# A windowed attention and a gated MLP on one core: GpSimd's loads put behind the last transposed x of a tile, key and query transposes a step later

## The chip, the core and the metric

The kernel runs on one core of a Trainium2 chip. The core has five engines with queues of their own: TensorE (PE, with its weight loads shown as PEld), VectorE (DVE), ScalarE (ACT), GpSimd (POOL) and SyncE (SP). Each executes its instructions in the order in which they were written; they meet through semaphores. GpSimd and SyncE also issue DMAs. The metric is the device time of one execution in microseconds. Before the change it is 281.39 us, the median of three runs between 280.98 and 281.63.

## What is computed

Windowed attention over 8 batches, 8 heads, 576 positions and 64 values a head, and then a two-layer MLP with the gate h * sigmoid(1.702 h) on its 4608 rows of 512:

```python
B, H, S, D = q.shape                      # 8, 8, 576, 64
scores = np.matmul(q, k.transpose(0, 1, 3, 2)) / np.sqrt(D)
mask = np.abs(pos[:, None] - pos[None, :]) <= 32
scores = np.where(mask, scores, -1e9)
attn = softmax(scores)
x = np.matmul(attn, v).transpose(0, 2, 1, 3).reshape(B * S, H * D)
h = x @ w_in                              # 512 -> 2048
out = (h * (1 / (1 + np.exp(-1.702 * h)))) @ w_out
```

Inputs and output are float32.

## The kernel before

The 4608 rows are cut into 36 units of 128 and 9 tiles of 512, so a tile is four units: tile t has units 4t to 4t+3. A unit's attention makes a row block x, and the MLP then works on a tile of x that is transposed (xT). Both MLP layers multiply 2x2 blocks with seven products in place of eight; `x_sums` makes the four sums of xT blocks that layer 1 needs, and `g_sums` those for layer 2. In `l1_group` product 1 reads a half of xT, and product 7, the next, reads the first sum that `x_sums` makes.

From tile 2 on the program is a loop over tiles, with `front(t)` and `back(t)` in turn; in both u = 4t + 4, the first unit of the tile behind.

- `front(t)` runs the scores of units u to u+3, the `x_sums` of tile t, and layer-2 work of the tile before.
- `back(t)` runs four groups (n = 0 to 3) of layer 1 of tile t, fills them with layer 2, and has the values of units u to u+3 in groups 1 and 3, with their division (`norm`) and their transposition into xT[t+1] (`x_T`, a DMA transpose that SyncE issues).

Everything that attention needs is loaded in `back` too, some units ahead, on two other queues:

- `fetch(u)` (GpSimd) issues the loads of q(u), k(u+1) and, from u = 18 on, v(u-1). The staging buffers of q and k are five deep, those of v nine. A load that crosses the end of a batch is issued in two pieces.
- `turn(u)` (SyncE) issues the DMA transposes of q(u) and k(u+1), which wait for those loads. The scores of unit u need q(u), k(u) and k(u+1) transposed.
- `spread(u)` (GpSimd) calls `odd_v(u)`, two copies that make a version of v shifted by 64 rows: the first takes the second half of v(u), the second the first half of v(u+1). The buffer `vo` that they write is one of three from unit 16 on, so the first copy waits for the values of unit u-3. The values of unit u need v(u) and this copy.

In each group the order of GpSimd's queue and of SyncE's is the order of these calls in `back`. For tile t > 3 it is, with one line a group:

```text
n=0: turn(u+4)  fetch(u+5)                          spread(u+2)
n=1: turn(u+5)  fetch(u+6)  x_T(u) x_T(u+1)         spread(u+3)
n=2: turn(u+6)  fetch(u+7)                          spread(u+4)
n=3: turn(u+7)  fetch(u+8)  x_T(u+2) x_T(u+3)       spread(u+5)
```

SyncE also issues the output stores, which come out of layer 2.

Of the kernel before, what the change touches and what calls it, by code (L numbers as in the profile page):

```python
# [17 lines left out]
F16 = mybir.dt.float16  # L18
# [5 lines left out]
TILE = 512  # L24


class _Kernel:
# [55 lines left out]
    def setup(self):  # L83
        nc, cst = self.nc, self.cst
        self.ident = cst.tile([128, 128], BF16, name="ident")
        self.identh = cst.tile([128, 128], F16, name="identh")
        self.mask = cst.tile([128, 4, SQ], BF16, name="mask")
        self.bias = cst.tile([128, 512], BF16, name="bias")
        self.w1 = cst.tile([128, 4, self.DFF], F16, name="w1")
        self.w2 = cst.tile([128, 16, self.DM], F16, name="w2")  # L90
        self.a = {i: cst.tile([128, 2, 1024], F16, name=f"a{i}") for i in (1, 2, 3, 4)}
        self.b = {i: cst.tile([128, 8, 256], F16, name=f"b{i}") for i in (1, 2, 3, 4)}
        self.k_first = cst.tile([128, 4, 64], BF16, name="k_first")
        self.v_first = cst.tile([64, self.H, 66], BF16, name="v_first")
        self.ve = [cst.tile([128, self.H, 66], BF16, name=f"ve{i}") for i in range(9)]
        self.vo = [cst.tile([128, self.H, 66], BF16, name=f"vo{i}") for i in range(5)]
        self.spark = cst.tile([128, 1], F32, name="spark")

    def setup_mask(self):

        D = self.work.tile([128, 128], F32, name="gap", tag="s7", bufs=2)
        self.nc.gpsimd.iota(D, pattern=[[-1, 128]], base=0, channel_multiplier=1,
                            allow_small_or_imprecise_dtypes=True)
        dve = self.nc.vector
        dve.tensor_single_scalar(self.ident, D, 0.0, op=ALU.is_equal)
        dve.tensor_copy(self.identh, self.ident)
        for r in (slice(0, 64), slice(64, 128)):
            d = D[r, r].rearrange("p (b s) -> p b s", b=1).to_broadcast([64, 2, SQ])
            up = int(r.start > 0)
            for blk, op in ((2 * up, ALU.is_ge), (2 - 2 * up, ALU.is_le)):  # L110
                dve.tensor_single_scalar(self.mask[r, blk:blk + 2, :], d, 0.0, op=op)
# [94 lines left out]
    def load_v(self, u, which=slice(None)):  # L206
# [3 lines left out]
        for off, b, s, n in list(self.pieces(128 * u, 128))[which]:  # L210
            self.nc.gpsimd.dma_start(t[off:off + n, :, :self.D], self.v[b, :, s:s + n, :].rearrange("h s d -> s h d"))  # L211

    def odd_v(self, u, eng, parts=(0, 1)):

        vo = self.vo[u % (3 if u > 15 else 5)]
        nxt = self.v_first if u == self.NU - 1 else self.ve[(u + 1) % 9][0:64]

        def words(ap):
            return ap.rearrange("p h d -> p (h d)").bitcast(I32)

        for i in parts:
            eng.tensor_copy(*((words(vo[64:128]), words(self.ve[u % 9][64:128])), (words(vo[0:64]), words(nxt)))[i])  # L222
# [88 lines left out]
    def values(self, u, tag):  # L311

        D = self.D
        p = self.p.pop(u)
        if tag == "t":
            acc = self.bank(tag, name="pv")
            self.acc[u] = [acc]
            acc = [acc[:, 0], acc[:, 1]]
        else:
            acc = [self.bank(x, name="pv") for x in tag]  # L320
            self.acc[u] = [x.rearrange("p (b n) -> p b n", b=1) for x in acc]
        for h in range(self.H):
            o = slice((h % 4) * (D + 1), (h % 4 + 1) * (D + 1))
            for blk in range(2):
                vt = (self.ve[u % 9], self.vo[u % (3 if u > 15 else 5)])[blk]
                w = p[:, h % 2, h // 2 * 2 + blk, :] if len(p.shape) == 4 else p[:, h % 2, h // 4, h // 2 % 2, blk, :]
                self.mm(acc[h // 4][64 * blk:64 * blk + 64, o], w, vt[:, h, :D + 1],
                        start=(h % 4 == 0))
# [423 lines left out]
    @staticmethod  # L752
    def do(fs, n=99):
        for _ in range(min(n, len(fs))):
            fs.pop(0)()
# [29 lines left out]
    def back(self, t):  # L785

        more = t + 1 < self.NT
        do, l2 = self.do, self.l2
        u = 4 * t + 4
        bands = [lambda i=i: self.band(u + i) for i in range(4)] if more else []  # L790
        dv = bands[0:2]
        for n in range(4):
            if (t, n) == (3, 1):
                self.turn(20)
            if (t, n) != (3, 0):
                self.turn(u + n + 4)
            if (t, n) not in ((2, 3), (3, 0), (3, 3)):
                self.fetch(u + n + 5)
            if t == 2 and n in (1, 3):
                self.values(u + n - 1, "t")  # L800
                self.norm(u + n - 1)
                self.x_T(u + n - 1)
            elif more and n in (1, 3):
                do(l2, self.AHEAD[n][0])
                self.values(u + n - 1, "AC")
                self.norm(u + n - 1)
                if u + n < self.NU - 1:
                    self.x_T(u + n - 1)
                self.values(u + n, "t")
                self.norm(u + n)  # L810
                self.x_T(u + n)
                do(l2, self.AHEAD[n][1])
            if (t, n) == (3, 0):
                self.fetch(20)
            self.spread(u + n + 2)
            if (t, n) == (3, 0):
                self.fetch(21)
            if (t, n) == (3, 3):
                self.fetch(24)

            key = ("first", n) if t == 2 else ("last", n) if not more else n
            share = dict(zip((1, 7, 2, 4), self.SHARES.get(key, (3, 3, 5, 5))))

            def fill(i):
                do(l2, share[i])
                self.l2eng = self.nc.scalar
                if t == 2 and n in (1, 3) and i == 7:
                    self.values(u + n, "t")
                    if n == 3:
                        self.norm(u + n)  # L830
                        self.x_T(u + n)
                if i == 4:
                    do(dv, 2 if (t, n) == (2, 2) else 99)

            def side(i):
                if (t, n, i) == (2, 1, 0):
                    self.norm(u + n)
                    self.x_T(u + n)
                else:
                    do(dv, 1)  # L840

            self.l1_group(t, n, fill, side)
            dv += bands[2:4] if n == int(t == 2) else []
            dv += self.g_sums(t, 2 * n, 2)
        return dv
# [132 lines left out]
```

## Time and profile before

| | |
|---|---|
| median of three runs | 281.39 us |
| the profiled execution | 281.27 us, of which the span from first to last instruction is 279.5 us |
| TensorE busy | 268.2 us (96% of the span) |
| VectorE, ScalarE busy | 210.9 us (75%), 195.4 us (70%) |
| GpSimd busy | 133.0 us (48%) |
| the chain that ended last | TensorE 90%, DMA 4%, GpSimd 3% |

The profile is one execution of the program, recorded by the hardware. Times are counted from the span's start. Views that group instructions show an engine, a line of the code, an operation and the tiles written and read (`vo<-ve`). A line can be that of a helper: every matmul has line 70. "Waits" lists how long an engine stood idle ahead of an instruction and what ended it. A DMA has a time of issue, which its queue spends, and a time "to landing", from its issue to its completion. TensorE's matmuls are pipelined, so that it counts as busy without gaps.

### The profile page before, as it was taken

The page shows a single profiled execution, that of the slowest core. Times are in us where ns is not written, and L with a number is a line of the kernel's source. Part 1 is how long each engine was busy: PE and PEld are TensorE (multiplying, and loading weights), DVE is VectorE, ACT ScalarE, POOL GpSimd, SP SyncE. Part 2 cuts the span into 40 slices and gives each one's busy share as a digit, 9 for nine tenths or more (in the row PEclk, how much of TensorE's full clock was granted, in tenths as well). Part 3 has the DMA queues.
Part 4 walks back from the last instruction along what each step waited for, and adds up shares of the span by engine and source line. Part 5 has one row for each costly group of instructions (what it writes and reads, how often), then busy time and mean ns, then how long its engine had stood idle before and what let it go on. Part 6 is the DMA issues. An engine that isn't in the chain of part 4 may idle for free.

```text
span 279.5 us, 8854 instructions
## 1 busy us (share of the span) xinstructions
PE 268.2 (96%) x3632; PEld 222.6 (80%) x3632; DVE 210.9 (75%) x491; ACT 195.4 (70%) x343; POOL 133.0 (48%) x199
## 2 busy tenths in 40 slices
PE   1989999999999999999999999999999999999995
PEld 1568656776888888888888888888888888888884
DVE  3454598897997798788888887888778887945731
ACT  2586893989897588758875877687759775568411
POOL 8894695999593554635684519442520100000000
PEclk9999999999999999999999999999999999999999
DMA  8999999999999999999999999999972050202023
GB/s 88 166 204 199 178 207 165 185 136 159 131 167 140 203 120 140 172 189 115 182 194 178 126 163 159 134 183 132 168 91 85 2 115 19 77 2 75 2 104 124
DMA packets 150265, 37.61 MB, mean 135 GB/s; under 512 B 138064, under 2 KB 145872, under 8 KB 150224
## 3 DMA queue, kind: packets, MB, share of 16 engines
q0 software_dynamic: 106656, 18.42, 95.5%
q1 hardware_dynamic: 43120, 18.10, 37.9%
q8 instruction: 28, 0.46, 0.7%
q10 hardware_dynamic: 448, 0.52, 0.6%
q14 instruction: 13, 0.11, 0.1%
HBM read 36.83 MB, written 9.44 MB: 166 GB/s over the span
## 4 chain that ended last, share of the span: by engine, by line
PE 90%; DMA 4%; POOL 3%; ACT 1%; issue 1%; POOLq 0%
PE o L70 41%; PE h L70 39%; PE pv L70 4%; DMA w<-in_moe_w_in_dram 4%; PE sc L70 3%; POOL ve L211 1%; POOL kq L152 1%; PE tp L201 1%; PE tp L244 1%; ACT p L279 1%; POOL w L125 1%; PE tp L368 0%; ACT kq L67 0%; PE tp L356 0%; ACT L692 0%
## 5 line engine op out<-in xcount | busy, mean ns | idle before, releaser
L471 ACT ACTIVATE g<-h 128x512 f16<-128x512 f32 x128 | 72.2, 598 | 35.0 <-PE h L70 34.8
L222 POOL COPY vo<-ve 64x264 int32<-64x264 int32 x71 | 32.7, 461 | 79.3 <-PE pv L70 52.0
L70 PEld LDWEIGHTS <-g 128*128 128x128 f16 x576 | 54.5, 98 | 10.1
L70 PE MATMUL h<-xs,a 128*128 128x256 f16 x384 | 57.6, 272 | 0.0
L70 PEld LDWEIGHTS <-a 128*128 128x128 f16 x512 | 49.5, 98 | 9.1
L70 PE MATMUL o<-w,g 128*128 128x256 f16 (+1 forms) x320 | 55.0, 294 | 0.0
L70 PEld LDWEIGHTS <-w 128*128 128x128 f16 x496 | 47.7, 98 | 7.6 <-DMA w<-in_moe_w_in_dram 0.2
L70 PE MATMUL h<-xT,w 128*128 128x256 f16 (+1 forms) x368 | 53.5, 277 | 0.1
L70 PEld LDWEIGHTS <-gs 128*128 128x128 f16 x384 | 36.7, 98 | 4.7
L70 PE MATMUL o<-b,g 128*128 128x256 f16 x256 | 38.3, 273 | 0.0
L70 PE MATMUL o<-b,gs 128*128 128x256 f16 x256 | 37.7, 273 | 0.0
L484 DVE TENSOR_TENSOR h<-h,s 128x512 f32<-128x512 f32 x32 | 22.4, 699 | 19.8 <-PE h L70 19.1
L211 POOL DMA_DIRECT2D ve<-in_v_dram x40 | 34.3, 864 | 5.6 <-DMA w<-in_moe_w_out_dram 2.1
L279 ACT ACTIVATE p<-sc 128x512 bf16<-128x512 f32 x64 | 32.8, 618 | 1.2 <-PE sc L70 1.0
L67 ACT COPY h<-h 128x512 f32<-128x512 f32 x32 | 18.8, 588 | 16.7 <-PE h L70 16.3
L340 DVE TENSOR_TENSOR x<-pv,rec 128x256 f16<-128x256 f32 (+1 forms) x52 | 27.4, 527 | 1.8
L141 POOL DMA_DIRECT2D qst<-in_q_dram x35 | 28.2, 809 | 0.3
L490 DVE TENSOR_TENSOR h<-h,s 128x512 f32<-128x512 f32 x32 | 22.4, 699 | 6.4 <-PE h L70 6.1
L141 POOL DMA_DIRECT2D kst<-in_k_dram x31 | 26.5, 855 | 0.8 <-DMA w<-in_moe_w_out_dram 0.8
L309 DVE TENSOR_TENSOR p<-p,mask 128x1024 bf16<-128x1024 bf16 x32 | 22.3, 696 | 0.2
L67 ACT COPY s<-h 128x512 f32<-128x512 f32 x32 | 19.2, 600 | 1.2
L70 PE MATMUL h<-xs,w 128*128 128x256 f16 x128 | 19.2, 273 | 0.0
(88 smaller groups left out, 343.2 us busy)
## 6 DMA issues: line engine op xcount, KB each, us to landing
out_dram<-o_sb SPq DMA_DIRECT2D x33, 256.0 KB, 4.6
ve<-in_v_dram POOLq DMA_DIRECT2D x32, 128.0 KB, 6.9
kst<-in_k_dram POOLq DMA_DIRECT2D x25, 128.0 KB, 6.5
qst<-in_q_dram POOLq DMA_DIRECT2D x21, 128.0 KB, 5.6
w<-in_moe_w_out_dram POOLq DMA_DIRECT2D x4, 512.0 KB, 11.0
w<-in_moe_w_in_dram POOLq DMA_DIRECT2D x3, 512.0 KB, 9.9
qst<-in_q_dram POOLq DMA_DIRECT2D x7, 96.0 KB, 5.7
kq<-in_q_dram POOLq DMA_DIRECT2D x2, 256.0 KB, 5.9
```

Of the source, the lines that this page charges most:

```text
L67: (eng.copy if eng is self.nc.scalar else eng.tensor_copy)(out, in_)
L70: self.nc.tensor.matmul(out, lhsT, rhs, start=start, stop=stop, skip_group_check=True)
L125: self.nc.gpsimd.dma_start(self.w1[:, :, lo:lo + n], self.w_in[:, lo:lo + n].rearrange("(k p) f -> p k f", p=128))
L141: self.nc.gpsimd.dma_start(t[off:off + n], src[b, :, s:s + n, :].rearrange("h s d -> s h d"))
L211: self.nc.gpsimd.dma_start(t[off:off + n, :, :self.D], self.v[b, :, s:s + n, :].rearrange("h s d -> s h d"))
L222: eng.tensor_copy(*((words(vo[64:128]), words(self.ve[u % 9][64:128])), (words(vo[0:64]), words(nxt)))[i])
L279: self.nc.scalar.activation(p[:, eo].rearrange("k h s -> k (h s)"), sc[eo], AF.Exp, scale=self.scale)
L309: (eng or self.nc.vector).tensor_mul(pv, pv, msk.to_broadcast([128, 8, 2, SQ]))
L340: dve.tensor_mul(x[:, 4 * at:4 * (at + n), :].rearrange("p (b h) d -> p b h d", b=n), acc[:, :, :, :D], r.to_broadcast([128, n, 4, D]))
L471: act.activation(g[:, f, 256 * half:256 * half + 256], bank.rearrange("p (i n) -> p i n", i=2), AF.Gelu_apprx_sigmoid)
L484: dve.tensor_add(e, b, s7)
L490: dve.tensor_add(c, b, s7)
```

## The change

A new one-element tile, `seen`, is written by GpSimd from the last column of xT[t], at the start of group 0 in `back(t)` for t > 2 as long as there are units to load. The copy waits for the last `x_T` of that tile, and everything behind it on GpSimd's queue follows it. Then come `fetch(u+4)` and `fetch(u+5)` together, and the other two fetches stand behind the `spread` of their group. On SyncE the transposes for unit u+4 move from group 0 to group 1, and those for u+5 stand behind x_T(u) and x_T(u+1). In tile 2 `fetch(19)` moves behind `spread(16)`. The special cases of tile 3 go. The odd buffers of units from 16 on are numbers 3, 4 and 0 in turn, where they were 0, 1 and 2. In the notation from above, for tile t > 2:

```text
n=0:            seen <- xT[t]  fetch(u+4) fetch(u+5)             spread(u+2)
n=1: turn(u+4)  x_T(u) x_T(u+1)  turn(u+5)                       spread(u+3)  fetch(u+6)
n=2: turn(u+6)                                                   spread(u+4)  fetch(u+7)
n=3: turn(u+7)  x_T(u+2) x_T(u+3)                                spread(u+5)
```

The orders of instructions on TensorE, VectorE and ScalarE stay as they were.

```diff
--- before.py
+++ after.py
@@ -95,6 +95,7 @@
         self.ve = [cst.tile([128, self.H, 66], BF16, name=f"ve{i}") for i in range(9)]
         self.vo = [cst.tile([128, self.H, 66], BF16, name=f"vo{i}") for i in range(5)]
         self.spark = cst.tile([128, 1], F32, name="spark")
+        self.seen = cst.tile([1, 1], F16, name="seen")
 
     def setup_mask(self):
 
@@ -210,9 +211,12 @@
         for off, b, s, n in list(self.pieces(128 * u, 128))[which]:
             self.nc.gpsimd.dma_start(t[off:off + n, :, :self.D], self.v[b, :, s:s + n, :].rearrange("h s d -> s h d"))
 
+    def odd(self, u):
+        return u % 5 if u < 16 else (3, 4, 0)[(u - 16) % 3]
+
     def odd_v(self, u, eng, parts=(0, 1)):
 
-        vo = self.vo[u % (3 if u > 15 else 5)]
+        vo = self.vo[self.odd(u)]
         nxt = self.v_first if u == self.NU - 1 else self.ve[(u + 1) % 9][0:64]
 
         def words(ap):
@@ -322,7 +326,7 @@
         for h in range(self.H):
             o = slice((h % 4) * (D + 1), (h % 4 + 1) * (D + 1))
             for blk in range(2):
-                vt = (self.ve[u % 9], self.vo[u % (3 if u > 15 else 5)])[blk]
+                vt = (self.ve[u % 9], self.vo[self.odd(u)])[blk]
                 w = p[:, h % 2, h // 2 * 2 + blk, :] if len(p.shape) == 4 else p[:, h % 2, h // 4, h // 2 % 2, blk, :]
                 self.mm(acc[h // 4][64 * blk:64 * blk + 64, o], w, vt[:, h, :D + 1],
                         start=(h % 4 == 0))
@@ -790,11 +794,9 @@
         bands = [lambda i=i: self.band(u + i) for i in range(4)] if more else []
         dv = bands[0:2]
         for n in range(4):
-            if (t, n) == (3, 1):
-                self.turn(20)
-            if (t, n) != (3, 0):
-                self.turn(u + n + 4)
-            if (t, n) not in ((2, 3), (3, 0), (3, 3)):
+            if t == 2 or n > 0:
+                self.turn(u + ((4, 5, 6, 7) if t == 2 else (0, 4, 6, 7))[n])
+            if t == 2 and n < 2:
                 self.fetch(u + n + 5)
             if t == 2 and n in (1, 3):
                 self.values(u + n - 1, "t")
@@ -810,13 +812,15 @@
                 self.norm(u + n)
                 self.x_T(u + n)
                 do(l2, self.AHEAD[n][1])
-            if (t, n) == (3, 0):
-                self.fetch(20)
+            if t > 2 and n == 0 and u + 4 <= self.NU:
+                self.nc.gpsimd.tensor_copy(self.seen, self.xT[t][0:1, 0, TILE - 1:TILE])
+                self.fetch(u + 4)
+                self.fetch(u + 5)
+            if t > 2 and n == 1:
+                self.turn(u + 5)
             self.spread(u + n + 2)
-            if (t, n) == (3, 0):
-                self.fetch(21)
-            if (t, n) == (3, 3):
-                self.fetch(24)
+            if n == 2 or t > 2 and n == 1:
+                self.fetch(u + n + 5)
 
             key = ("first", n) if t == 2 else ("last", n) if not more else n
             share = dict(zip((1, 7, 2, 4), self.SHARES.get(key, (3, 3, 5, 5))))
```

## The prediction

> **What bounds the kernel now.** I read the waits of TensorE first, then the busy time by tile, then the queues of GpSimd and SyncE around one tile, and last the landing times of single transfers. These are all of TensorE's waits in the whole run:
>
> ```profile
> PE tp L177 <- DVE ve L623: 6.3, 1, 6.3
> PE tp L356 <- ACT p L300: 0.8, 1, 0.8
> PE tp L356 <- DVE x L340: 0.4, 2, 0.3
> PE sc L70 <- DVE kq L67: 0.2, 1, 0.2
> ```
>
> All four name lines of the opening. In the tiles where the change stands, TensorE waits for nothing. The busy times by tile, cut from one tile's first score matmul to the next tile's (columns: stretch, its length, then busy time and count for each engine, granted clock, DMA share, GB/s), say the same:
>
> ```profile
> core 0: us, PE busy (x) PEld busy (x) DVE busy (x) ACT busy (x) POOL busy (x), PEclk, DMA share, GB/s
> ...
> 128.02:155.66 27.64, 27.64 (x385) 23.90 (x384) 23.31 (x56) 20.69 (x37) 16.88 (x26) 1.00 2.28 168
> ...
> 210.94:238.58 27.64, 27.64 (x386) 24.16 (x386) 22.98 (x56) 20.69 (x37) 0.81 (x2) 1.00 0.23 54
> ```
>
> A tile takes 27.64 us with the DMA rings crowded (2.28) and with them nearly empty (0.23). So what the change might relieve, loads and transposed x on the same rings, costs TensorE nothing today. The change can only lose, by letting something arrive after TensorE wants it. What it wants in the front of a tile (t = 5; columns: start, length, engine, line, operation):
>
> ```profile
> 155.66 0.70 PE L70 MATMUL sc<-qT,kT 64*64 64x64 bf16 x48
> ...
> 158.58 0.70 PE L70 MATMUL sc<-qT,kT 64*64 64x64 bf16 x48
> ...
> 161.41 0.60 PE L70 MATMUL h<-xs,a 128*128 128x256 f16 x4
> ```
>
> ```profile
> 160.16 0.42 DVE L400 TENSOR_TENSOR xs<-xT 128x512 f16<-128x512 f16 x1
> ```
>
> Call 155.66 the tile's zero. The last two units' scores start at +2.9. Product 7 reads the first x_sum at +5.75. That sum takes 0.42 and needs all of xT, so the last transposed x has to land by about +5.2 (0.1 for the hand-over).
>
> **The change part by part.** Units 20 to 23 are tile 4's back, u = 20. Before, GpSimd runs ahead of the tiles: `fetch(25)` to `fetch(28)` alternate with `spread(22)` to `spread(25)`, and each `spread` needs a v that was issued one `fetch` earlier. After, for t > 2, GpSimd's queue reads: `seen` (waits for the last transposed x of xT[t]), `fetch(u+4)`, `fetch(u+5)`, `spread(u+2)`, `spread(u+3)`, `fetch(u+6)`, `spread(u+4)`, `fetch(u+7)`, `spread(u+5)`, next `seen`. The second copy of `spread(u+3)` reads v(u+4), which is the very last load issued in front of it; that of `spread(u+4)` reads v(u+5), issued just before; and so on. So `fetch(u+6)` can't start before v(u+4) has landed, nor `fetch(u+7)` before v(u+5). On SyncE `turn(u+7)` still stands ahead of the transposes of x(u+2) and x(u+3), and its second DMA waits for k(u+8) out of `fetch(u+7)`. The last x then releases the next `seen`. Behind `seen` stand all later loads and odd copies, for which SyncE's transposes and TensorE's values wait; behind a late x_sum stand VectorE's copies of layer 2, which TensorE wants in the same front. That is a closed loop from tile to tile: last x, two loads, v lands, loads, v lands, loads, k lands, transposes, last x. Its length L, beside 27.64 us, decides.
>
> Queue costs today. GpSimd:
>
> ```profile
> 143.03 0.51 POOL L222 COPY vo<-ve 64x264 int32<-64x264 int32 x1 [0.29 <-DMA ve<-in_v_dram]
> 143.49 0.89 POOL L141 DMA_DIRECT2D qst<-in_q_dram  x1
> 144.37 0.88 POOL L141 DMA_DIRECT2D kst<-in_k_dram  x1
> 145.23 0.90 POOL L211 DMA_DIRECT2D ve<-in_v_dram  x1
> ...
> 167.29 1.35 POOL L141 DMA_DIRECT2D qst<-in_q_dram  x2
> ```
>
> SyncE:
>
> ```profile
> 147.54 1.26 SPq L235 DMA_TRANSPOSE qT<-qst  x1
> 148.90 1.21 SPq L235 DMA_TRANSPOSE kT<-kst  x1
> 151.42 2.54 SPq L352 DMA_TRANSPOSE xT<-x  x2
> ```
>
> A load costs GpSimd 0.87 (143.49 to 144.37), a q or k that crosses a batch 1.35; the copy that follows a landing holds the queue 0.46 (143.03 to 143.49), with 0.12 for the wake-up 0.58. SyncE spends 1.3 on a transpose.
>
> Landing times, each from a view of one tile cut to a few us: v in the opening's burst of loads; v with little else in flight; then one v issued at 125.5 among transposes; and one k issued at 140.5.
>
> ```profile
> L211 POOL DMA_DIRECT2D ve<-in_v_dram x5: 730/896/911, 5.2 to 8.6; - x5
> ...
> DMA to landing us min/median/max: 6.2/6.5/6.7
> ```
>
> ```profile
> L211 POOL DMA_DIRECT2D ve<-in_v_dram x2: 876/890/903, 45.8 to 48.4; - x2
> ...
> DMA to landing us min/median/max: 5.2/5.4/5.6
> ```
>
> ```profile
> DMA to landing us min/median/max: 7.5/7.5/7.5
> ```
>
> ```profile
> DMA to landing us min/median/max: 5.2/5.2/5.2
> ```
>
> Transposed x with no load in flight, and with loads:
>
> ```profile
> L352 SPq DMA_TRANSPOSE xT<-x x2: 1192/1204/1217, 206.7 to 208.0; - x2
> ...
> DMA to landing us min/median/max: 2.4/2.4/2.4
> ```
>
> ```profile
> L352 SPq DMA_TRANSPOSE xT<-x x2: 1192/1222/1251, 151.4 to 152.7; - x2
> ...
> DMA to landing us min/median/max: 4.6/5.9/7.1
> ```
>
> The loop of tile 4, from the landing of x(19). `seen` is a copy of one element; no row has it, it lies between nothing and the 0.46 of a copy, I take 0.25 with its wake-up. Five issues at 0.87 follow: v24 is issued at 4.6. It lands 6.0 later (between 5.2 and 7.5; it is the sixth of a burst, so nearer to 6.5 than to 5.2, with fewer loads in front than the opening had): 10.6. Copy, 11.2. q26 and k27, 12.9: v25 is issued and lands 5.5 later, a burst of three: 18.4. Copy, 19.0. q27, then k28 is issued at 19.9 and lands 5.2 later: 25.1. SyncE issues kT28 at 25.2, x(22) at 26.5, x(23) at 27.8. It lands 3.2 later (2.4 with clear rings; v26 is still in flight, against 7.1 with many loads): **L = 31.0**, 3.4 over the tile.
>
> Loads that cross a batch lengthen the other loops by 0.5 each before the loop's next step: k22 and q22 in tile 3, k31 and q31 in tile 5. In tile 3 the two output stores go out just ahead of the first loads, which I put at another 0.5. Tile 6 has one such v, but no k36; its last q has two pieces: 31.0 again. Tiles 3 to 6: 32.5 + 31.0 + 32.0 + 31.0 = 126.5, against 4 x 27.64 = 110.6. **15.9 over.** From tile 7 on only one v is left to load and nothing waits.
>
> The start has room. Before, x(15) lands here:
>
> ```profile
> 100.39 0.70 PE L70 MATMUL sc<-qT,kT 64*64 64x64 bf16 x48
> ```
>
> ```profile
> L352 SPq DMA_TRANSPOSE xT<-x x2: 1217/1241/1265, 96.4 to 97.7; - x2
> ...
> DMA to landing us min/median/max: 5.3/5.6/6.0
> ```
>
> That is 97.7 + 6.0 = 103.7, 3.3 after tile 3's zero of 100.39. After, the next loads, which today start while x(15) is in flight, come only behind it; I take 102.5, +2.1. It may land at +5.2, so 3.1 of the excess is free (1.9 if it lands as today). Loss: 15.9 - 3.1 = **12.8 us**. The profiled execution took 281.27 us (span 279.5), 0.12 under the median of 281.39: 281.27 + 12.8 = 294.1, forecast **294.0**. With the quickest landings shown (5.2, 5.2, 5.2, 2.4) L is 29.1 and the loss 118.9 - 110.6 - 3.1 = 5.2: 286.5. With the medians of today's whole run for all:
>
> ```profile
> ve<-in_v_dram POOLq DMA_DIRECT2D x32, 128.0 KB, 6.9
> kst<-in_k_dram POOLq DMA_DIRECT2D x25, 128.0 KB, 6.5
> ```
>
> and 5.9 for x, L is 37.3, 151.7 in all, and the loss 151.7 - 110.6 - 1.9 = 39: 320.
>
> The other edits cost nothing: the odd buffers rotate over three as before, and a copy into one waits for the values of three units earlier, which in tile 4 (20 and 21) run at 138.3, before the v that the copy needs lands. `fetch(19)` moves behind `spread(16)`, whose second copy waits for v17 until 88.2 (the chain of waits, then the queues of GpSimd and SyncE):
>
> ```profile
> 138.30 0.66 PE pv L70 x32
> ```
>
> ```profile
> 88.23 1.11 POOL L222 COPY vo<-ve 64x264 int32<-64x264 int32 x2 [2.84 <-DMA ve<-in_v_dram]
> ```
>
> ```profile
> 95.05 1.21 SPq L235 DMA_TRANSPOSE kT<-kst  x1
> ```
>
> k20 is then issued at 89.6 and lands at 95 (5.2) to 96, when SyncE wants it today: 0 to 1 us on x(15), which is part of the choice of 102.5. `turn(u+5)` behind x(u+1) is wanted only in the next tile.
>
> The Trainium skill ("DMA: Bandwidth & Descriptors", Anatomy of one DMA) gives a GpSimd load as 2.0 us plus its bytes at 436 GB/s: an estimate of 2.6 us for the 256 KB read here. By that L would be some 21 us and nothing would be lost; the whole-unit rows, 5.2 and up, disagree.
>
> **The rivals.**
> - *Loads land early enough* (not slower). L under 28.4 loses less than the 3.1 free: 281.3, no change. It needs three landings of 5.0 at most, x in 2.4 and no crossing cost. For it: landings today are stretched by transposes that will now stand apart. Against it: 5.2 with little else in flight.
> - *A gain.* x lands some 3 us sooner and VectorE no longer waits. An x_sum has waited for xT once in the run:
>
> ```profile
> DVE xs L400 <- DMA xT<-x: 0.4, 1, 0.4
> ```
>
> Even if all of that reached TensorE, which has no such wait, it would be 280.9.
> - *Crowded landings stay.* The loads of a tile are squeezed into less of it, two bursts meet the stores; nearer to the medians, L of 34 to 37: 305 to 320.
> - *The clock falls in the new gaps.* After the last matmul the rows show this:
>
> ```profile
> 276.20:278.60 2.40, 0.00 (x0) 0.00 (x0) 0.00 (x0) 0.33 (x1) 0.00 (x0) 1.00 0.54 177
> 278.70:279.40 0.70, 0.00 (x0) 0.00 (x0) 0.00 (x0) 0.00 (x0) 0.00 (x0) 0.50 0.04 12
> ```
>
> 2.6 us idle, then half clock. A stall of 3.4 us could do the same. If the slow time lasts as long as the stall, TensorE loses 1.7 us a tile; but the tile then takes 29.3, still under L, so the next stall shrinks by as much, and only the last one adds: 295.7. The Trainium skill ("TensorE: Matmul & The Clock Gate", What's actually happening) has half rate after an idle window of about 3.4 us, so by that rule gaps of this size are at the edge.
>
> **How the numbers follow.** Forecast with L of 29 to 34 (286 to 305): 0.66. Clock as well: 0.08. Crowded: 0.14. Loads early enough: 0.08. A gain: 0.04. About 0.2% is what a measurement of this kernel can tell from no change. So slower 0.88, same 0.08, faster 0.04. The range of 285 to 310 leaves out the last two cases and half of the crowded one.
>
> **What would show it.** Right: TensorE waits once a tile in the fronts of tiles 4 to 7, at product 7 or the last scores, some 2 to 5 us each, for VectorE's x_sum or a DMA; GpSimd waits for v two or three times a tile; tiles 3 to 6 take 30 to 33 us, tiles 7 and 8 as before. The forecast is wrong if the fronts show no wait, if v lands 4 us after issue, or if the last x goes out before k(u+8) has landed.

## The result, and the profile after

| | before | after |
|---|---|---|
| median (lowest to highest) of six runs | 281.23 us (280.98 to 281.63) | 297.15 us (296.46 to 301.14) |
| the profiled execution, its span | 281.27 us, 279.5 us | 296.56 us, 294.8 us |

The changed kernel takes 1.0563 of the time before, with a 95% interval of 1.0538 to 1.0588. Some executions take some per cent longer than the quickest of the same kernel; ratios leave them out, here and below, and where too few others are left, there is no ratio, and the median and range of all runs are given. The two profiled executions differ by 15.3 us in their spans, and this is the difference that the rest explains. From the page of the kernel after come TensorE's busy time and the chain that ended last, by engine:

```profile
PE 272.4 (92%) x3632; PEld 223.6 (76%) x3632; DVE 211.1 (72%) x491; ACT 196.4 (67%) x343; POOL 134.0 (45%) x204
...
PE 84%; DVE 6%; DMA 5%; ACT 2%; issue 2%; POOL 1%; SPq 0%; POOLq 0%; DVEq 0%
```

TensorE fell from 96% to 92% of the span, and the chain goes through other engines for 16% of it. The waits of TensorE between 100 and 262 us, where the kernel before had none, and GpSimd's of the whole run (us in total, times, the longest):

```profile
PE h L70 <- DVE xs L404: 5.7, 4, 1.9
PE sc L70 <- DMA qT<-qst: 2.3, 3, 1.0
PE sc L70 <- DMA kT<-kst: 2.3, 3, 1.0
PE sc L70 <- ACT p L283: 0.2, 1, 0.2
```

```profile
POOL vo L226 <- DMA ve<-in_v_dram: 52.6, 19, 5.1
POOL seen L816 <- DMA xT<-x: 26.5, 5, 5.6
POOL vo L226 <- PE pv L70: 8.8, 5, 3.3
```

TensorE waits for the first x_sum four times and for a transposed q or k three times each. GpSimd waits 52.6 us for values in flight and 26.5 at the new gate. Cut at each tile's first score matmul, tiles 3 to 6 read (stretch, length, busy time and count of PE, PEld, DVE, ACT and POOL, granted clock, DMA share, GB/s):

```profile
100.03:127.67 27.64, 27.64 (x385) 23.94 (x384) 23.46 (x57) 20.58 (x36) 14.79 (x22) 1.00 1.40 134
127.67:159.32 31.65, 28.42 (x385) 24.05 (x384) 23.13 (x56) 20.96 (x37) 15.03 (x24) 1.00 1.33 135
159.32:190.63 31.31, 28.42 (x385) 24.06 (x385) 23.07 (x56) 20.95 (x37) 13.98 (x22) 1.00 1.25 133
190.63:222.75 32.12, 30.09 (x386) 24.85 (x385) 23.47 (x56) 20.95 (x37) 15.15 (x24) 0.95 1.34 135
```

Tile 3 is as before. Tiles 4, 5 and 6 lose 4.0, 3.7 and 4.5 us against 27.64, together 12.2. Tile 3 starts 0.4 earlier than before (100.03, not 100.39), and the remaining 3.5 of the 15.3 fall behind 222.75, most of them in tile 7's front. The waits add up to only 10.5 us. Much of the rest stands as busy time: with the same number of matmuls a tile is busy for 28.42 where it was 27.64. No matmul is recorded longer for that (the mean of a 64x64 score matmul is 194 ns in both kernels' tile 4), but the records of neighbours overlap, and at a wait that overlap is missing: the 48 score matmuls that took 0.70 us in one go (158.58 before) take 0.45, 0.24 and 0.44 in three pieces below. In tile 6 the clock fell for a while as well (below). So a list of waits understates a stall. What a stall looks like, in tile 5's front (PE, then DVE; start, length, operation, and in brackets the idle time before it with what ended it):

```profile
162.24 0.45 PE L70 MATMUL sc<-qT,kT 64*64 64x64 bf16 x24
163.10 0.24 PE L70 MATMUL sc<-qT,kT 64*64 64x64 bf16 x2 [0.42 <-DMA qT<-qst]
163.98 0.44 PE L70 MATMUL sc<-qT,kT 64*64 64x64 bf16 x22 [0.63 <-DMA kT<-kst]
...
168.47 0.61 PE L70 MATMUL h<-xs,a 128*128 128x256 f16 x4 [1.76 <-DVE xs L404]
```

```profile
167.99 0.42 DVE L404 TENSOR_TENSOR xs<-xT 128x512 f16<-128x512 f16 x1 [4.10 <-DMA xT<-x]
```

Product 7 waits 1.76 us for a sum that VectorE starts at 167.99, as soon as the last transposed x is there. Before, that sum started 4.5 us behind its tile's zero; now it is 8.7 (167.99 less 159.32). Why x is late stands on GpSimd's queue (tile 4, then the gate of tile 5) and on SyncE's:

```profile
136.63 0.18 POOL L816 COPY seen<-xT 1x1 f16<-1x1 f16 x1 [5.63 <-DMA xT<-x]
137.12 0.89 POOL L142 DMA_DIRECT2D qst<-in_q_dram  x1 [0.31 <-issue]
...
141.46 0.93 POOL L212 DMA_DIRECT2D ve<-in_v_dram  x1
...
146.72 0.40 POOL L226 COPY vo<-ve 64x264 int32<-64x264 int32 x1 [2.43 <-DMA ve<-in_v_dram]
147.22 1.36 POOL L142 DMA_DIRECT2D qst<-in_q_dram  x2
...
149.43 0.91 POOL L212 DMA_DIRECT2D ve<-in_v_dram  x1
...
155.78 0.40 POOL L226 COPY vo<-ve 64x264 int32<-64x264 int32 x1 [4.99 <-DMA ve<-in_v_dram]
156.23 0.88 POOL L142 DMA_DIRECT2D qst<-in_q_dram  x1
157.10 0.89 POOL L142 DMA_DIRECT2D kst<-in_k_dram  x1
```

```profile
167.95 0.18 POOL L816 COPY seen<-xT 1x1 f16<-1x1 f16 x1 [4.96 <-DMA xT<-x]
```

```profile
161.65 1.19 SPq L239 DMA_TRANSPOSE kT<-kst  x1
162.93 2.53 SPq L356 DMA_TRANSPOSE xT<-x  x2
```

From one gate to the next it is 31.32 us (167.95 less 136.63), and each step starts where the one before it ends: gate, v issued at 141.46, its copy at 146.72, the next loads behind that copy, v issued at 149.43, its copy at 155.78, k issued at 157.10, its transpose at 161.65, the two x, gate. The gates stand at 103.40, 136.63, 167.95, 200.06 and 230.94, so 33.2, 31.3, 32.1 and 30.9 apart. TensorE needs 27.64 for a tile and follows.

### The profile page after: what moved, and what is told of

Its sections match the earlier page's. It is cut to its first block, busy times and chain, and to the rows that moved or that the text cites. A ratio compares the mean times of both kernels' runs of the same rounds, so it can differ in the third digit from the quotient of the medians.

```text
span 294.8 us, 8859 instructions
## 1 busy us (share of the span) xinstructions
PE 272.4 (92%) x3632; PEld 223.6 (76%) x3632; DVE 211.1 (72%) x491; ACT 196.4 (67%) x343; POOL 134.0 (45%) x204
## 4 chain that ended last, share of the span: by engine, by line
PE 84%; DVE 6%; DMA 5%; ACT 2%; issue 2%; POOL 1%; SPq 0%; POOLq 0%; DVEq 0%
PE h L70 37%; PE o L70 36%; DMA xT<-x 5%; PE pv L70 4%; PE sc L70 4%; DVE xs L404 1%; PE tp L178 1%; PE tp L202 1%; PE tp L248 1%; POOL kq L153 1%; DVE o L67 1%; ACT p L283 1%; DVE gs L419 1%; DVE o L568 1%; ACT p L304 1%
## 5 line engine op out<-in xcount | busy, mean ns | idle before, releaser
L70 PEld LDWEIGHTS <-g 128*128 128x128 f16 x576 | 54.8, 98 | 10.5
L70 PEld LDWEIGHTS <-a 128*128 128x128 f16 x512 | 48.9, 98 | 17.1 <-DVE xs L404 8.2
L226 POOL COPY vo<-ve 64x264 int32<-64x264 int32 x71 | 32.1, 453 | 64.0 <-DMA ve<-in_v_dram 52.6
L70 PE MATMUL o<-b,gs 128*128 128x256 f16 x256 | 38.5, 277 | 0.0
```

What stands on the lines that cost most here:

```text
L70: self.nc.tensor.matmul(out, lhsT, rhs, start=start, stop=stop, skip_group_check=True)
```

## The experiments

"Loss" below is the median less that of the kernel before in the same comparison.

**1. The changed kernel without its gate.**

```diff
-                self.nc.gpsimd.tensor_copy(self.seen, self.xT[t][0:1, 0, TILE - 1:TILE])
                 self.fetch(u + 4)
```

> The change without the copy that waits for the last x; GpSimd's loads follow one another as the change orders them. Closed loop: the link from x back to the loads is cut. GpSimd's own chain from one tile's first load to the next one's took 25.9 to 27.1 us in the changed kernel's trace, under the 27.64 of a tile, so nothing is lost: 281 to 283 us; if loads land later again because x flies among them, three landings of 7 us make that chain some 30 us and cost up to 8: at most 290. Rival, the parts add up (gate, order of loads, order on SyncE each with a share of the 15.9 us): about 292.

It took 299.7 us (294.03 to 303.24; before 281.98). The runs lie far apart, but the quickest of them is still 13 us above the quickest of the kernel before (281.07), and 2.4 below the quickest of the kernel after. So the gate isn't what most of the time hangs on. GpSimd's queue in tile 4:

```profile
134.29 0.92 POOL L212 DMA_DIRECT2D ve<-in_v_dram  x1
...
145.50 0.87 POOL L226 COPY vo<-ve 64x264 int32<-64x264 int32 x2 [7.03 <-PE pv L70]
146.32 1.36 POOL L142 DMA_DIRECT2D qst<-in_q_dram  x2
...
148.54 0.90 POOL L212 DMA_DIRECT2D ve<-in_v_dram  x1
...
155.49 0.67 POOL L226 COPY vo<-ve 64x264 int32<-64x264 int32 x1 [5.47 <-DMA ve<-in_v_dram]
156.11 0.88 POOL L142 DMA_DIRECT2D qst<-in_q_dram  x1
```

v(24) is issued 7 us earlier than in the kernel after (134.29, not 141.46), but the fetch at 146.32 starts hardly sooner (147.22 there): it stands behind copies that wait for an odd buffer, which TensorE's values free, and for v(24), issued at 134.29, which lands 10.1 us later by its record, at 144.4. The two waits end about a us apart, and which of them would hold it alone wasn't tried. So the loop closes another way: product 7, values, copy, loads, v lands, loads, k lands, x, product 7. Values in flight during a tile's work (104 to 200 us) show the price of the missing gate:

```profile
L212 POOL DMA_DIRECT2D ve<-in_v_dram x14: 707/901/935, 104.1 to 199.4; - x14
...
DMA to landing us min/median/max: 3.7/6.8/10.4
```

The same view of the kernel after:

```profile
L212 POOL DMA_DIRECT2D ve<-in_v_dram x13: 715/908/945, 105.6 to 190.2; - x13
...
DMA to landing us min/median/max: 3.7/4.5/6.4
```

With the gate loads and transposed x are apart and the median of a landing is 2.3 us lower, but GpSimd spends about 5 us idle at each gate. With or without it the tile is too short.

**2. Each fetch of groups 1 and 2 ahead of its spread,** the gate kept.

```diff
-            self.spread(u + n + 2)
             if n == 2 or t > 2 and n == 1:
                 self.fetch(u + n + 5)
+            self.spread(u + n + 2)
```

> The change with the loads of groups 1 and 2 ahead of the odd copies of their group, the gate and SyncE's order kept. Closed loop: fetch(u+6) waits no more for v(u+4), nor fetch(u+7) for v(u+5), so one landing of some 6 us leaves the loop, L falls from 31 to 32 us to about 25, under the tile: 281 to 282.5 us. Rival, parts add up: about 292. Rival, the gate alone starves TensorE (the loads start too late whatever their order): 290 or more.

281.6 us (281.5 to 282.36), ratio 0.9979 (0.9951 to 1.0007): the whole loss is gone. GpSimd's waits between 100 and 240 us:

```profile
POOL seen L816 <- DMA xT<-x: 28.6, 5, 7.2
POOL vo L226 <- PE pv L70: 18.5, 5, 7.1
POOL vo L226 <- DMA ve<-in_v_dram: 13.1, 13, 2.2
```

It waits for the gate as long as the kernel after does, and TensorE waits for nothing. What went is the wait for v: the load that has just been issued has one more group of loads behind it before the queue stops for it.

**3. The last transposes of q and k behind the last two x on SyncE,** so that x doesn't wait for k(u+8).

```diff
-            if t == 2 or n > 0:
+            if t == 2 or n in (1, 2):
...
-            if t > 2 and n == 1:
-                self.turn(u + 5)
+            if t > 2 and n in (1, 3):
+                self.turn(u + (5 if n == 1 else 7))
```

> The change with the transposes for unit u+7 behind those of x(u+2) and x(u+3) on SyncE; GpSimd's queue is the change's. Closed loop: x waits no more for k(u+8). The last x lands about when the next tile begins, the gate opens then, GpSimd's chain of 26 to 27.5 us from gate to gate just fits the tile, and the last key lands 3 us before its scores: 281 to 284 us. Rival, parts add up: about 292. Rival, GpSimd's serial landings are the cost by themselves: 295 or more.

291.67 us (289.16 to 293.52), ratio 1.0315 (1.0242 to 1.0387): about 6 of the 16 us saved, a miss. The gates are 28.4, 30.0, 32.0 and 29.7 apart, and GpSimd hardly waits at them (100 to 240 us):

```profile
POOL vo L226 <- DMA ve<-in_v_dram: 57.4, 15, 6.1
POOL vo L226 <- PE pv L70: 8.2, 2, 4.8
POOL seen L816 <- DMA xT<-x: 5.0, 1, 5.0
```

x isn't what the queue is late for: GpSimd's own chain, now with three values landing in series a tile (the third for the copy of `spread(u+5)`), is longer than a tile by itself in this trace. Each landing is also longer here: 5.9 us at the median (v, 104 to 200 us), where the kernel after has 4.5. I had taken the step through x for a necessary one.

**4. The gate alone,** in the kernel before, from tile 3 on; and **5. the changed order of SyncE alone.**

```diff
+            if t > 2 and n == 0 and u + 4 <= self.NU:
+                self.nc.gpsimd.tensor_copy(self.seen, self.xT[t][0:1, 0, TILE - 1:TILE])
```

> The kernel before with only the copy that waits for the last x, in front of group 0's load from tile 3 on; all orders as before, one load group ahead of the copies. Closed loop: there is a gate, but the last load whose transposes stand ahead of x is issued some 8 us after the gate, so the loop is some 20 us, under the tile: 281 to 282 us. Rival, the gate alone starves TensorE or parts add up: 286 to 296.

284.31 us (284.18 to 284.86), ratio 1.0087 (1.0056 to 1.0118): 2.3 us lost, where none was expected. Most of it lies in tile 4, which is 30.29 us long: the special cases of tile 3 put five fetches behind that tile's gate, between 103.73 and 130.5, so that the next x and the next gate (135.97) came late. **Experiment 10** therefore gates from tile 4 on (`t > 3`):

> The kernel before with the gate from tile 4 on only (with it from tile 3 on it took 284.3, all of it lost in one tile, since five fetches had to follow tile 3's gate). Closed loop: from tile 4 on four fetches follow a gate and the last one's transposes stand in the next tile, so no loss: 281 to 282 us. Rival (the gate costs something wherever it stands): 283 to 285.

281.48 us (280.97 to 283.02), ratio 0.9988 (0.9968 to 1.0008). In this kernel a gate costs nothing and brings nothing where the loads of a tile get through behind it.

```diff
-            if (t, n) == (3, 1):
-                self.turn(20)
-            if (t, n) != (3, 0):
-                self.turn(u + n + 4)
+            if t == 2 or n > 0:
+                self.turn(u + ((4, 5, 6, 7) if t == 2 else (0, 4, 6, 7))[n])
...
+            if t > 2 and n == 1:
+                self.turn(u + 5)
```

> The kernel before with SyncE's order of the change (transposes of units u+4 and u+5 in group 1, the latter behind x), GpSimd's queue as before. Closed loop: no gate, and these transposes are wanted only in the next tile: 281 to 282 us, no change. Rival, parts add up: the SyncE part alone costs some us, 284 to 288.

285.43 us (284.22 to 286.92), ratio 1.0117 (1.0053 to 1.018): a loss of 3.9. SyncE in tile 4:

```profile
151.48 1.22 SPq L235 DMA_TRANSPOSE qT<-qst  x1
152.80 1.97 SPq L235 DMA_TRANSPOSE kT<-kst  x1
154.86 2.56 SPq L352 DMA_TRANSPOSE xT<-x  x2
```

The two x leave at 154.86, where they left at 151.42 before: the late transposes and a store stand in front of them. Product 7 waits for them twice, 2.2 us in all, and the tiles take 27.8 to 29.3. So the rival was right here.

**6 and 7. A dose: four copies of 64x264 words behind the gate of the kernel after, and at the same place of the kernel before.** They write a tile that nothing reads, and hold GpSimd for 1.84 us by the 0.46 of a copy; in the traces four of them take 1.8 to 2.4.

```diff
+                for _ in range(4):
+                    self.nc.gpsimd.tensor_copy(self.dose.rearrange("p h d -> p (h d)").bitcast(I32), self.v_first.rearrange("p h d -> p (h d)").bitcast(I32))
```

> The change with four copies of 64x264 words on GpSimd right behind the gate, 0.46 us each, 1.8 us in all, that nothing reads. Closed loop: GpSimd's queue is a link of the loop, so four loops grow by 1.8 us each: 297 + 7.4 = 304 us (303 to 306). Rival, the time is lost in landings and waits beside GpSimd's queue, which is idle for 64 us before its copies: the copies fall into idle time, 297 to 299.

> The kernel before with the same four copies at the same place, at the start of group 0 from tile 3 on. Control: GpSimd runs ahead and has idle time, so no change on either theory: 281 to 282 us. If it is slower, GpSimd's queue is short of time by itself, and the dose in the change says less.

After: 303.79 us (300.01 to 305.82), ratio 1.0681 (1.0574 to 1.0788), 6.6 more than the changed kernel's 297.15 (7.4 for four gates by the dose). By the ratios it is 3.3 more, and their intervals touch, so the size is loose. The trace, of an execution of 305.82, shows where it goes: four doses hold GpSimd for 9.1 us, and the four loops from the gate at 103.27 to that at 239.84 take 136.6, 9.0 more than the kernel after needs from 103.40 to 230.94. Before: 281.28 us (280.7 to 282.9), ratio 0.9981 (0.9957 to 1.0006). GpSimd waits for over 80 us in the kernel after and is busy for 45% of the span, and yet work that it gets on top lengthens the run, while the kernel before takes the same work for nothing. That is what a closed loop looks like, and no view of busy shares shows it.

**8. Only the order of loads and copies,** in the kernel before: no gate, SyncE as it was but for `turn(u+4)`, which stands behind its fetch.

```diff
+            if t > 2 and n == 0 and u + 4 <= self.NU:
+                self.fetch(u + 4)
+                self.fetch(u + 5)
+                self.turn(u + 4)
...
-            if (t, n) == (3, 0):
-                self.fetch(20)
             self.spread(u + n + 2)
-            if (t, n) == (3, 0):
-                self.fetch(21)
-            if (t, n) == (3, 3):
-                self.fetch(24)
+            if n == 2 or t > 2 and n == 1:
+                self.fetch(u + n + 5)
```

> The kernel before with the change's order of loads and odd copies on GpSimd alone: no gate, SyncE's order as before (turn(u+4) in group 0 waits for its loads). Theory as mended by the runs so far (each fetch behind a copy that waits for the v issued just before: three landings in a row are the cost, gate or no gate): slower by as much as without the gate, 291 to 300 us. Rival (it takes the late transposes on SyncE too): 281 to 285 us.

297.26 us (291.33 to 298.09; before 281.04): this part alone makes a loss of 16.2 by the median, and of 10.3 by the quickest run. Tile 4 on GpSimd:

```profile
145.12 0.86 POOL L222 COPY vo<-ve 64x264 int32<-64x264 int32 x2 [8.33 <-PE pv L70]
145.94 1.36 POOL L141 DMA_DIRECT2D qst<-in_q_dram  x2
...
154.20 0.40 POOL L222 COPY vo<-ve 64x264 int32<-64x264 int32 x1 [4.57 <-DMA ve<-in_v_dram]
```

The second of these copies waits for a v in flight, as forecast. The first stand where they stood in experiment 1, but here v(24), issued at 133.19, lands 8.8 us later, at 142.0, and they start at 145.12, behind TensorE's values of unit 20, which run from 144.52. So in this tile the odd buffer holds the fetch, and not the landing. More odd buffers weren't tried.

**9. Loads first as in experiment 2, and no gate.**

> The change with the loads of groups 1 and 2 ahead of the odd copies and without the gate; SyncE's order is the change's. The kernel before with that SyncE order alone took 285.4, the same with gate and loads first 281.6. Theory that the gate is what mends SyncE's order (it keeps the loads out of the way of x): 284 to 287 us. Rival (the gate does nothing, the new place of the loads mends it): 281 to 282.5.

284.06 us (282.6 to 285.42), ratio 1.0105 (1.0054 to 1.0155), beside 0.9979 with the gate. Here the gate is worth something. With SyncE's new order x leaves late, and these are the landings of transposed x between 104 and 240 us, first here, then in experiment 2:

```profile
DMA to landing us min/median/max: 2.4/5.9/7.6
```

```profile
DMA to landing us min/median/max: 2.4/4.0/7.0
```

With the gate a quicker landing makes up for the late start; without it 3.0 us are lost, about what experiment 5 lost by the order alone (3.9).

**11. The dose in experiment 2's kernel.**

> The change with the loads of groups 1 and 2 ahead of the odd copies, and four copies (1.84 us) on GpSimd behind the gate. In the trace without the dose the gates open 28.3 us apart in tile 4 (130.32, 158.63), so the loop is near the tile's 27.64 and the last x of tile 5 lands some 2 us before it is late. Closed loop: with 1.84 more it is past the tile and each of four tiles loses 1 to 2 us after the first 2 are used up: 283 to 289 us. Rival (GpSimd waits 28.6 us at its gates, which swallows the dose): 281 to 282.

286.73 us (283.89 to 293.03), ratio 1.0167 (1.0094 to 1.0239). That kernel runs at the speed of the one before, with 28.6 us of GpSimd's time spent waiting at gates, and still the dose is felt: its loop has less to spare than the dose takes (1.9 to 2.4 us in the trace). The kernel before, where GpSimd runs ahead of the tiles, took the same dose for nothing.

**12. In the kernel after, v issued first in a fetch,** ahead of q and k.

```diff
+        if u >= 20:
+            self.load_v(u - 1)
         self.load_kq("q", u)
```

> The change with v issued ahead of q and k within each fetch from unit 20 on, else as it is. Three landings of v are in the loop and each v is issued 1.74 us sooner after what it waits for (two of them between gate and fetch(u+7)), the last k 0.87 later: L falls by 1.74 + 1.74 - 0.87 = 2.6 us a tile, from the measured 33.2, 31.3, 32.1, 30.9 to a sum of 117.1, and the loss from 15.3 to some 5 us: 284 to 289. Rival (it is the landings' number that counts, or bandwidth, not what stands between): 294 to 298.

288.6 us (282.27 to 289.8; before 281.04): by the median about half of the loss is gone, but one run lost only 1.2 us and the other three 7.3 to 8.8, so how much it is stays open. Each v is issued earlier by the two issues that stood in front of it, and k later by one. In the trace, of the run of 289.8, the gates are 31.8, 30.4, 29.7 and 29.3 apart, 121.2 in all where 117.1 was expected.

No version beats the kernel before by more than the measurement can tell: experiments 2, 7 and 10 have intervals that hold 1, and in their traces TensorE waits for nothing between 100 and 262 us; a tile from tile 4 on takes 27.6 to 27.7 us in all three.

## Why the prediction was right, and where it wasn't

**What bounds, and the sign.** Right. With TensorE full, the change could only lose, and did. The stalls stand in the fronts of tiles 4 to 7, at product 7 and the last scores, as forecast; each wait is shorter than the 2 to 5 us named, 1.9 at most, since a tile's loss of 3.5 to 4.5 is spread over two or three waits and the overlap of matmuls that is missing at each. By the cut that the prediction had quoted, tiles 4 to 7 are the long ones, not 3 to 6: a loop that begins in tile 3 stalls TensorE in tile 4.

**The size.** The loss was put at 12.8 us and is 15.3. Tile 4's loop, step by step, each measured from the start of one row shown above to the start of the next (the predicted step has the 0.12 of a wake-up or 0.1 of a hand-over with it):

| step | predicted | measured |
|---|---|---|
| gate to first load | 0.25 | 0.49 |
| five issues to v(24) | 4.35 | 4.34 |
| v(24) to its copy | 6.12 | 5.26 |
| copy | 0.46 | 0.50 |
| q(26), k(27) to v(25) | 1.74 | 2.21 |
| v(25) to its copy | 5.62 | 6.35 |
| copy, and q(27) to k(28) | 1.33 | 1.32 |
| k(28) to its transpose | 5.3 | 4.55 |
| transpose of k(28), two x, last lands, gate | 5.8 | 6.30 |
| sum | 31.0 | 31.3 |

The errors offset one another. One is a slip: q(26) crosses a batch, and its second piece (1.36 for two) was put into no loop of tile 4. All four loops add up to 127.5 us (230.94 less 103.40), where 126.5 was predicted. The term that was mis-sized is the start: x(15) was taken to land at 102.5 once no load is in flight with it, and it landed 0.85 later, at 103.35, just ahead of the gate at 103.40. The landing itself was quick, 2.5 us, but the issue was late, at 100.9 where it had been 97.7: SyncE's transposes follow one another without room from 84.33 on, where SyncE got a k that took 7.6 us to land (4.6 before), and why that load was slower stays open. Tile 3 also began at 100.03 and not at 100.39. The free room was 100.03 + 5.2 - 103.35 = 1.9, the other value that the prediction had worked out, and not 3.1. 127.5 - 110.6 - 1.9 = 15.0 of the 15.3 us.

**The mechanism.** "That is a closed loop from tile to tile" was right for the kernel after, and the doses show it. But the loop was described as if the gate made it, and experiment 1 shows that this was wrong: without the gate some 13 us or more are lost. What is necessary is the order of the other sentence, "`fetch(u+6)` can't start before v(u+4) has landed, nor `fetch(u+7)` before v(u+5)": turning that order round removes the whole loss (experiment 2), and bringing it alone into the kernel before makes a loss of 10 us or more (experiment 8). In the kernel after the fetches wait for v, as the sentence says (146.72 and 155.78 above). Without the gate the copy in front of a fetch also waits for its odd buffer, and in tile 4 of experiment 8 that alone holds it. So it is the place of the fetch behind a copy that waits, by whichever of the two waits ends last; their shares weren't separated. Once GpSimd's loads are strung behind such copies, some path closes in about 30 us: by the gate, by TensorE's values (experiment 1), or on GpSimd alone (experiment 3). The place of x behind k(u+8) is worth about 6 us of the 16.

**The edits put at nothing.** "`turn(u+5)` behind x(u+1) is wanted only in the next tile" judged a moved step by who wants its own result and overlooked what stands behind it on SyncE: alone the new order costs 3.9 us (experiment 5). Whether it costs anything on top of GpSimd's loop in the kernel after wasn't tried; without the gate, experiments 1 and 8 differ by little else, and their losses are 17.7 and 16.2, with runs several us apart. The copies into the odd buffers wait for no values in tile 4 of the kernel after, as said, but do so when the gate is gone (145.50 above): the cover was the gate.

**The rivals.** Loads that land early enough didn't come: v took 4.5 us at the median and 6.4 at worst (104 to 200 us), and the two in tile 4's loop 5.1 and 6.2. The 2.6 us that the Trainium skill's formula gives ("DMA: Bandwidth & Descriptors", Anatomy of one DMA) were reached by no v of this kernel, of which the quickest took 3.3. The gain didn't come either, nor in experiments 2 and 10, where TensorE waits for nothing and the time stays. Crowded landings went the other way: between 104 and 200 us the median of v fell from 7.0 in the kernel before to 4.5. The clock did fall, once, in tile 6 (columns as above; then TensorE around it):

```profile
196.17:199.58 3.41, 3.41 (x17) 2.37 (x18) 0.00 (x0) 1.08 (x2) 0.00 (x0) 0.50 0.81 87
```

```profile
194.90 0.24 PE L70 MATMUL sc<-qT,kT 64*64 64x64 bf16 x2 [0.90 <-DMA qT<-qst]
195.72 0.44 PE L70 MATMUL sc<-qT,kT 64*64 64x64 bf16 x22 [0.58 <-DMA kT<-kst]
...
200.59 0.61 PE L70 MATMUL h<-xs,a 128*128 128x256 f16 x4 [0.47 <-DVE xs L404]
```

At half speed for 3.41 us TensorE loses 1.7, and its next wait at product 7 is 0.47 where tile 5's was 1.76: the stall behind it took the loss in, as that rival had worked out, and the gates stay 30.9 to 32.1 apart.

## What to carry to other kernels

A DMA issue that stands in a queue behind an instruction that waits for an earlier DMA puts that DMA's whole landing time, 5 to 6 us here, in series with it. A wait for a buffer that another engine must free does the same with that engine's work. Count the landings that a queue goes through in one round and compare the sum with the round of the engine that bounds. Keep at least one group of loads issued ahead of the copy that waits for the last one. Idle time of an engine is no measure of its room once it sits in such a loop: a small dose of work at the suspected place, in both kernels, tells.

## What the runs showed of the hardware beyond that

The same load of v lands 4.5 us after its issue at the median when transposed x is kept out of its way, and 6.8 with the two mixed, up to 10.4, in kernels that move the same bytes (kernel after and experiment 1). The gate isn't the whole of it: behind the same gate, with the loads of experiment 2, the median is 6.0.

The clock fell to half behind two waits of TensorE of 0.90 and 0.58 us, and held at full speed in tile 5 (granted clock 1.00) through 0.63 and 1.76. The Trainium skill ("TensorE: Matmul & The Clock Gate", What's actually happening) has the half rate after an idle window of some 3.4 us: the half-speed stretch has that length here (3.41), but the waits ahead of it come to less than half of it.
